# Attention into two feed-forward layers: scores and folds as tiles of the array, low weight bits on ScalarE

## Chip, cores and metric

One core of one Trainium2 chip runs the whole program. The metric is device microseconds for one execution, start to end; a smaller number is better. Engines: PE is TensorE (PEld its weight loads), DVE VectorE, ACT ScalarE, POOL GpSimd, SP the queue that issues nearly all DMAs.

## What is computed

```python
def _attn_ref(x, state):            # x (4,8,512,64), state (4,8,32,64)
    scale = 1.0 / np.sqrt(D)
    scores = scale * np.matmul(x, state.transpose(0, 1, 3, 2))
    scores = scores - scores.max(-1, keepdims=True)
    a = np.exp(scores)
    a /= a.sum(-1, keepdims=True) + 1e-09
    xread = np.matmul(a, state)
    scores2 = scale * np.matmul(state, x.transpose(0, 1, 3, 2))
    ...                             # the same softmax, over the 512 tokens
    sread = np.matmul(a2, x)
    return np.concatenate([xread, sread], axis=2)

h = X @ w_in1;  X2 = elu(h) @ w_out1            # X: (2304, 512)
h = X2 @ w_in2; out = (h * tanh(softplus(h))) @ w_out2
```

w_in is 512 x 2048 and w_out 2048 x 512, in both layers. They arrive as float64 and are read as pairs of 32-bit words.

## The kernel before

**Order.** The program hands some 1,800 operations to a planner (`Plan`, line 63). Each has an engine, a cost, a due time and the buffers it needs; `run` picks the next one by its own clock, so the order on each engine is fixed when the program is built. On the chip each engine and each DMA queue works strictly in that order.

**Weights** (`weight`, line 414). A piece of 128 x 512 float64 lands in `raw`. ACT scales the high words into `wy` (L446). DVE shifts `wy` left by three into `wv` (L455), ors in the top three bits of the low words (L457), and ors in the sign bit (L468, L474 or L478). There are 64 pieces, `raw_in` and `raw_out` of either layer. Most are then split into a rounded fp32r part and a remainder (`split_weight`, line 488), since the large products are made of three fp32r matmuls (L769 to L771, L849 to L851). The first eight steps of layer 1 use whole fp32 instead (L755, L837).

**Folds** (`fold`, line 509). For the tokens, attention output times w_in1 is written as probabilities times (state times w_in1). A fold makes `m`, state times w_in1, for one batch b and four pieces j. The array is cut into eight tiles of 64 x 32, one for each pair of head group and state half; a matmul covers two pieces (256 columns), so four pieces take two groups of eight products, which the planner may place apart. `m` leaves PSUM as fp32, and `fold_slice` (line 537) splits each piece of it into two halves of the tile `ms`, three steps before its use.

**Tokens** (`token_reads`, line 571), for each batch and half of the heads: x is turned on PE (L600), scores are eight 128-row products with a block-diagonal state `sd` of 64 columns (L638), softmax runs on DVE and ACT (L648 to L658), the probabilities are turned on PE (L663) and become `x1`. The raw scores go to DRAM (`s2d`, L654).

**States** (`state_reads`, line 674): the raw scores come back by DMA, x is loaded a second time with a column of ones (L566), a maximum over the tokens is taken on DVE (L685) and POOL (L686), and PE reads (L697).

**Stages.** Layer 1 works through four batches in sixteen steps each, with the 128 state rows as four more; layer 2 then has five blocks of rows, sixteen steps each. PE has eight PSUM banks: two `h`, four `acc`, two `att`, the last shared by everything of the attention and the folds. During the start (`early`) the others serve too.

```python
A("PE", 0.9, score, r=[(xT, q), ("sd", b, 0), ("sd", b, 1)], w=[(pt, q)], lag=lag, place=held)
add("ACT", 0.68, lambda: nc.scalar.activation(y.t, words()[0].bitcast(F32), AF.Copy, scale=2.0 ** -112),
add("DVE", 0.43, lambda: nc.vector.tensor_scalar(u32(v), u32(y), 3, None, ALU.logical_shift_left),
```

Of the kernel before, what the change touches and what calls it, by code (L numbers as in the profile page):

```python
# [40 lines left out]
class Buf:  # L41
# [7 lines left out]
    def __getitem__(self, i):  # L49
        return self.t[i]  # L50

# [5 lines left out]
class Plan:  # L57
# [59 lines left out]
    def run(self, take, dma):  # L117

        self.dues(dma)
        free = {}  # L120
# [15 lines left out]
        while todo:  # L136
# [52 lines left out]
            c = op.cost[e] if isinstance(op.cost, dict) else op.cost  # L189
            if e in dma:  # L190
# [25 lines left out]
def attention_elu_mish(  # L216
# [39 lines left out]
    negative = const.tile([P, 1], F32, name="negative")  # L256
    x2d = pools["dram"].tile([P, NK, NT * P], F32, name="x2d")
    w2d = pools["dram"].tile([P, 2, NF, DM], F32, name="w2d")
    s2d = pools["dram"].tile([P, B, 2, NC, P], F32, name="s2d")
# [77 lines left out]
    add("DVE", 2.8, make_ident, w=["ident"], due=-50.0)  # L337
    add("POOL", 0.1, lambda: nc.gpsimd.memset(one, 1.0), w=["one"], due=-50.0)
    add("POOL", 0.1, lambda: nc.gpsimd.memset(two, 2.0), w=["two"], due=-50.0)
    add("POOL", 0.1, lambda: nc.gpsimd.memset(negative, -0.0), w=["negative"], due=-50.0)  # L340

    banks = itertools.cycle(["att", "acc0", "att", "acc1", "h", "acc2", "h"] + ([] if FILL else ["acc3"]))
    early = True

    def bank(name):
        tag = next(banks) if early else "att"
# [17 lines left out]
    sd = [pools["at"].tile([P, 2, HH, 2, NS], F32, name=f"sd{b}") for b in range(B)]  # L364
# [11 lines left out]
    def load_states():  # L376
        raw = buf("w", "w_out", NF, [P, 2 * B, 2, D], F32, "st_raw")
        for i in range(2):
            A(ACTQ, 128.0, lambda i=i: nc.scalar.dma_start(
                out=raw[:, :, i, :], in_=state.rearrange("b (g h) n d -> (h n) (b g) d", g=2)),  # L380
              w=[(raw, i)], due=-50.0)
        for b in range(B):
            A("POOL", 0.5, lambda b=b: nc.gpsimd.memset(sd[b], 0.0), w=[("sd", b, i) for i in range(2)], due=-50.0 + b)
        st_raw.append(raw)

    def states(b0, b1):

        raw = st_raw[0]
        if True:
# [8 lines left out]
            for b in range(b0, b1):  # L398
                for i in range(2):
                    r = slice(i * D, (i + 1) * D)  # L400
                    A(EITHER, {"ACT": 0.41, "DVE": 0.43}, lambda e, b=b, b0=b0, i=i, r=r, pt=pt: copy(
                        e, sd[b][r, :, :, i, :],
                        pt[r, (b - b0) * 2 * P:(b - b0 + 1) * 2 * P].rearrange("p (g h n) -> p g h n", g=2, n=NS)),
                        r=[pt], w=[("sd", b, i)])
# [4 lines left out]
    def place_w1(j, k):  # L409
        return w1[j // 2].t.rearrange("p (k f) -> p k f", k=NK)[:, k, j % 2 * P:(j % 2 + 1) * P]  # L410
# [3 lines left out]
    def weight(kind, layer, j, due=None):  # L414
# [33 lines left out]
        signs = layer == 1 and Z_FROM <= j < Z_TO  # L448
        if signs:

            add("ACT", 0.68, lambda: nc.scalar.activation(v.t, y.t, AF.Identity, bias=negative, scale=2.0 ** -60),
                r=[y, "negative"], w=[v])
        else:

            add("DVE", 0.43, lambda: nc.vector.tensor_scalar(u32(v), u32(y), 3, None, ALU.logical_shift_left),  # L455
                r=[y], w=[v])
        add("DVE", 0.69, lambda: nc.vector.scalar_tensor_tensor(  # L457
            u32(v), words()[1], 29, u32(v), ALU.logical_shift_right, ALU.bitwise_or), r=[raw, v], w=[v])
        last = (3, ALU.logical_shift_left) if signs else (0x80000000, ALU.bitwise_and)
        if kind == "in" and layer == 1:  # L460
            if j // 2 not in w1:
                w1[j // 2] = buf("w", "w_in", NF, [P, NK * 2 * P], F32, f"w1_{j // 2}_")
            to = w1[j // 2]

            def sign():
                o = to.t.bitcast(U32).rearrange("p (k f) -> p k f", k=NK)[:, :, j % 2 * P:(j % 2 + 1) * P]
# [3 lines left out]
            add("DVE", 0.69, sign, r=[y, v], w=[(to, j % 2)])  # L470
            return
        if layer == 1 and j < WHOLE_OUT:
            w = w_sb["whole", layer, j] = buf("w", f"w_{kind}", NF, [P, DM], F32, f"whole{j}_")
# [12 lines left out]
    after_step = {}  # L486

    def split_weight(kind, layer, j, v):
        w = w_sb[kind, layer, j] = buf("w", f"w_{kind}", NF, [P, 2, DM], F32R, f"w_{kind}{layer}_{j}_")
# [573 lines left out]
```

## Time and profile before

| what | value |
|---|---|
| time, three runs | 752.93, 753.81, 754.55 us |
| span of the profiled execution, first to last instruction | 751.1 us |
| median less that span | 2.7 us |
| PE busy | 732.6 us, 98% |
| DVE, ACT, POOL busy | 556.8, 425.0, 10.6 us |
| moved by DMA | 81.71 MB |

The profiled execution's own time isn't listed beside the three, so the span stands for it and the 2.7 us for what lies around it. Busy time says how long an engine had something running; the chain of waits says which engine ended last at each moment.

### The profile page before, as it was taken

To read this page: it belongs to the slowest core of one execution; us is meant where nothing else is said; L and a number is where in the kernel's file an instruction comes from. 1 tells how busy PE (TensorE), PEld (TensorE's weight loads), DVE (VectorE), ACT (ScalarE), POOL (GpSimd) and SP (SyncE) were. 2 spreads that over 40 slices of the span, in tenths; PEclk is the share of its full clock that TensorE was granted. 3 is DMA by queue.
4 is the path that set the end of the run, shared out by engine and by line. 5 is a ranking of instruction groups with operands and counts; after the bars stand their busy time and mean duration, and the time that the engine had idled before them with its cause. 6 is when DMAs were issued, how large, how long until landed. Compare 5 with 4: busy or idle time off the path is not lost.

```text
span 751.1 us, 11051 instructions
## 1 busy us (share of the span) xinstructions
PE 732.6 (98%) x4098; PEld 598.0 (80%) x4098; DVE 556.8 (74%) x1048; ACT 425.0 (57%) x759; POOL 10.6 (1%) x27
## 2 busy tenths in 40 slices
PE   5899999999999999999999999999999999999996
PEld 5346677788777879878888888888889999999995
DVE  6988899988689895798999856565567565756564
ACT  3674767655567663577657445454455455545443
POOL 1000000010000000000000000000000000000000
PEclk8899999999999999999999999999999999999999
DMA  9953667453585543665845103000030020001001
GB/s 227 291 154 101 166 161 215 117 169 113 147 256 175 189 140 104 189 196 185 283 162 193 42 1 99 0 1 1 0 99 1 1 83 2 1 1 42 1 1 42
DMA packets 67292, 81.71 MB, mean 109 GB/s; under 512 B 22696, under 2 KB 45992, under 8 KB 67240
## 3 DMA queue, kind: packets, MB, share of 16 engines
q1 hardware_dynamic: 65028, 80.36, 36.1%
q10 hardware_dynamic: 2212, 0.66, 0.4%
q8 instruction: 32, 0.52, 0.3%
q14 instruction: 20, 0.16, 0.1%
HBM read 59.51 MB, written 21.50 MB: 108 GB/s over the span
## 4 chain that ended last, share of the span: by engine, by line
PE 94%; DMA 2%; DVE 1%; ACT 1%; issue 0%; SPq 0%; ACTq 0%
PE acc_acc L849 16%; PE acc_acc L851 15%; PE acc_acc L850 15%; PE h L769 12%; PE h L771 12%; PE h L770 12%; PE fold L523 2%; PE acc_acc L837 2%; PE h L745 2%; PE h L755 2%; DMA raw_in<-in_moe_w_in 2%; PE scores L638 1%; PE pT L663 1%; PE sr L697 1%; DMA xb<-in_x 1%; PE xT L600 1%
## 5 line engine op out<-in xcount | busy, mean ns | idle before, releaser
L788 ACT ACTIVATE e<-h 128x512 f32<-128x512 f32 (+1 forms) x148 | 83.2, 562 | 118.2 <-PE h L771 106.5
L813 ACT CAST g<-e 128x512 fp32r<-128x512 f32 (+1 forms) x142 | 82.4, 581 | 61.9 <-PE acc_acc L851 25.6
L771 PE MATMUL h<-x,w_in 128*128 128x384 f32 (+1 forms) x320 | 114.6, 358 | 0.0
L769 PE MATMUL h<-x,w_in 128*128 128x384 f32 (+1 forms) x320 | 114.4, 358 | 0.0
L770 PE MATMUL h<-x,w_in 128*128 128x384 f32 (+1 forms) x320 | 114.3, 357 | 0.0
L814 DVE TENSOR_TENSOR g<-e,g 128x512 fp32r<-128x512 f32 (+1 forms) x142 | 91.1, 642 | 22.5 <-ACT g L813 21.7
L851 PE MATMUL acc_acc<-w_out,g 128*128 128x512 f32 x272 | 106.9, 393 | 0.0
L850 PE MATMUL acc_acc<-w_out,g 128*128 128x512 f32 x272 | 106.7, 392 | 0.0
L849 PE MATMUL acc_acc<-w_out,g 128*128 128x512 f32 x272 | 105.9, 389 | 0.4 <-ACT g L813 0.4
L849 PE MATMUL acc_acc<-g,w_out 128*128 128x512 f32 x232 | 93.3, 402 | 0.0
L810 DVE TENSOR_TENSOR u<-u,e 128x384 f32<-128x384 f32 (+1 forms) x80 | 48.9, 611 | 57.7 <-ACT e L809 57.6
L850 PE MATMUL acc_acc<-g,w_out 128*128 128x512 f32 x232 | 90.5, 390 | 0.0
L851 PE MATMUL acc_acc<-g,w_out 128*128 128x512 f32 x232 | 90.5, 390 | 0.0
L808 ACT ACTIVATE e<-u,two 128x384 f32<-128x384 f32 (+1 forms) x80 | 52.8, 660 | 50.1 <-DVE u L806 49.9
L805 DVE TENSOR_SCALAR e<-e 128x384 f32<-128x384 f32 (+1 forms) x80 | 30.9, 387 | 48.2 <-ACT e L788 48.1
L769 PEld LDWEIGHTS h<-x,w_in 128*128 128x128 f32 x320 | 60.1, 188 | 7.1
L770 PEld LDWEIGHTS h<-x,w_in 128*128 128x128 f32 x320 | 60.1, 188 | 7.1
L771 PEld LDWEIGHTS h<-x,w_in 128*128 128x128 f32 x320 | 60.1, 188 | 5.0
L851 PEld LDWEIGHTS acc_acc<-w_out,g 128*128 128x128 f32 x272 | 51.0, 187 | 11.0 <-DVE g L814 0.3
L849 PEld LDWEIGHTS acc_acc<-w_out,g 128*128 128x128 f32 x272 | 51.1, 188 | 10.1 <-ACT g L813 0.9
L850 PEld LDWEIGHTS acc_acc<-w_out,g 128*128 128x128 f32 x272 | 51.0, 188 | 9.5
L849 PEld LDWEIGHTS acc_acc<-g,w_out 128*128 128x128 f32 x232 | 43.5, 188 | 13.5 <-issue 3.3
(126 smaller groups left out, 1169.7 us busy)
## 6 DMA issues: line engine op xcount, KB each, us to landing
raw_out<-in_moe_w_out SPq DMA_DIRECT2D x32, 512.0 KB, 4.3
raw_in<-in_moe_w_in SPq DMA_DIRECT2D x32, 256.0 KB, 7.3
raw_in<-in_moe_w_in SPq DMA_DIRECT2D x16, 512.0 KB, 4.2
w2d<-wv SPq DMA_DIRECT2D x32, 256.0 KB, 3.4
xb<-in_x SPq DMA_DIRECT2D x16, 256.0 KB, 4.2
x2d<-o SPq DMA_DIRECT2D x16, 256.0 KB, 2.6
xb<-in_x SPq DMA_DIRECT2D x32, 128.0 KB, 3.9
back_in<-w2d SPq DMA_DIRECT2D x16, 256.0 KB, 3.0
```

The source lines that it names most:

```text
L769: nc.tensor.matmul(h[:, :n], lhsT=wh, rhs=xh, start=(k == 0), stop=False)
L770: nc.tensor.matmul(h[:, :n], lhsT=wh, rhs=xl, start=False, stop=False)
L771: nc.tensor.matmul(h[:, :n], lhsT=wl, rhs=xh, start=False, stop=(k == nk - 1))
L788: add("ACT", act(n), lambda: nc.scalar.activation(E(), Hh(), AF.Exp), r=[h], w=[e])
L805: add("DVE", 0.1 + 0.00065 * n, lambda: nc.vector.tensor_scalar(E(), E(), E20, None, ALU.min), r=[e], w=[e])
L808: add("ACT", act(n) + 0.12, lambda: nc.scalar.activation(E(), U(), AF.Ln, bias=two), r=[u, "two"], w=[e])
L810: add("DVE", dve(n), lambda: nc.vector.tensor_tensor(U(), U(), E(), ALU.mult), r=[u, e], w=[u])
L813: add("ACT", act(n) + 0.01, lambda: nc.scalar.copy(g[:, 0, :n], E()), r=[e], w=[(g, 0)])
L814: add("DVE", dve(n), lambda: nc.vector.tensor_tensor(g[:, 1, :n], E(), g[:, 0, :n].bitcast(F32), ALU.subtract), r=[e, (g, 0)], w=[(g, 1)])
L849: nc.tensor.matmul(acc.t, lhsT=st[:, 0, :], rhs=mv[:, 0, :], start=fst, stop=False)
L850: nc.tensor.matmul(acc.t, lhsT=st[:, 0, :], rhs=mv[:, 1, :], start=False, stop=False)
L851: nc.tensor.matmul(acc.t, lhsT=st[:, 1, :], rhs=mv[:, 0, :], start=False, stop=lst)
```

## The change

- **Weights**: ACT makes the low three bits from the low words, as integers (`wv`), beside `wy`. DVE's shift by three goes; DVE ors sign and low bits, then the shifted `wy`.
- **Folds**: `w1` is laid out in fours, and a fold is one group of eight products of 512 columns. For all but the first eight steps it leaves PSUM as a rounded copy and a DVE subtraction from PSUM (L549 of the new kernel); `fold_slice` goes.
- **Scores**: eight products on tiles of 64 x 32, each 256 columns wide. Turns of 32 x 32 blocks on DVE (L620, L625, L640, L646) replace PE's turn of the probabilities.
- **States**: the raw scores and x stay in SBUF, so `s2d`, the second load of x, the ones and POOL's reduction go. One DVE maximum, POOL's 128x1 scaling, one ACT exponential that also sums, and a PE turn (L673) of the result with its copy come in. State copies are 4 of 128x256 in place of 8 of 64x256.
- **Planner**: other constants and gates for state reads, a start offset, and slower PE costs in its first 16 us; `w_in`, `w_wide` and `w_out` buffers are cut otherwise.

```diff
+        add("ACT", 0.68, lambda: nc.scalar.activation(
+            u32(v), words()[1], AF.Copy, bias=-0.5, scale=2.0 ** -29 * (1 - 2.0 ** -20)), r=[raw], w=[v])
         add("DVE", 0.69, lambda: nc.vector.scalar_tensor_tensor(
-            u32(v), words()[1], 29, u32(v), ALU.logical_shift_right, ALU.bitwise_or), r=[raw, v], w=[v])
-        last = (3, ALU.logical_shift_left) if signs else (0x80000000, ALU.bitwise_and)
+            u32(v), u32(y), 0x80000000, u32(v), ALU.bitwise_and, ALU.bitwise_or), r=[y, v], w=[v])
+        last = (3, ALU.logical_shift_left)
...
-        step = min(2, j1 - j0)
+        step = j1 - j0
...
+            A(EITHER, both(n), lambda g, e=e: copy(g, ms[0][:, e, :], pts[e].t), r=[(pts[e], j0)], w=[(ms[0], e)])
+            A("DVE", 0.69, lambda e=e: nc.vector.tensor_tensor(
+                ms[1][:, e, :], pts[e].t, ms[0][:, e, :].bitcast(F32), ALU.subtract),
+              r=[(pts[e], j0), (ms[0], e)], w=[(ms[1], e)], lag=0.5)
-        add(EITHER, {"ACT": 0.41, "DVE": 0.33}, lambda e: copy(e, t[:, 0], src()), r=keys, w=[(t, 0)])
-        add("DVE", 0.43, lambda: nc.vector.tensor_tensor(t[:, 1], src(), t[:, 0].bitcast(F32), ALU.subtract),
...
+        def score_tiles():
+            for h in range(HH):
+                for t in range(2):
+                    r, l = slice(t * D, (t + 1) * D), slice(h * NS, (h + 1) * NS)
+                    nc.tensor.matmul(ps[t][l, 0:2 * P], lhsT=sd[b][r, hf, h, :],
+                                     rhs=xT[r, h // 2, h % 2 * 2 * P:(h % 2 + 1) * 2 * P],
+                                     start=True, stop=True, tile_position=(t * D, h * NS))
...
+            if early:
+                A("DVE", 0.43, lambda t=t: nc.vector.transpose(
+                    pr()[:, t * 2 * P:(t + 1) * 2 * P], ps[t][:, 0:2 * P]), r=[ps[t]], w=[(kp, t)])
+            A(EITHER, both(2 * P), lambda e, t=t: copy(e, krv()[:, t, :], ps[t][:, 0:2 * P]), r=[ps[t]], w=[krk(t)],
...
+            A("DVE", 0.69, lambda: nc.vector.transpose(pr(), krv().rearrange("p t f -> p (t f)")),
...
-        A(SP, 256.0, lambda: nc.sync.dma_start(out=s2d[:, b, hf], in_=raw()), r=[kr], w=[("s2d", b, hf)])
...
-        A("PE", NC * 0.11, turn2, r=["ident", kp], w=[p2], lag=lag, place=[xt])
+        back = lambda o, i: nc.vector.transpose(
+            o.rearrange("p (c t f) -> p t c f", c=2, t=2), i.rearrange("p (t c f) -> p t c f", t=2, c=2))
...
-        xb = load_x_ones(b, hf)
+        xb, raw, rawk = kept.pop((b, hf))
...
-        A("POOL", 1.2, lambda: nc.gpsimd.partition_all_reduce(tot.t, col.t, P, RMAX), r=[col], w=[tot], lag=1.0)
+        A("POOL", 0.3, lambda: nc.gpsimd.tensor_scalar(top.t, top.t, SCALE, None, ALU.mult), r=[top], w=[top])
+        A("ACT", 0.8, lambda: nc.scalar.activation(
+            raw(), raw(), AF.Exp, bias=top.t, scale=SCALE, accum_out=den.t), r=[top],
+        A("PE", NC * 0.11, turn, r=["ident", *rk], w=[pe], lag=1.0, place=[exT])
+        A(EITHER, both(S), lambda e: copy(e, exT.t.rearrange("p c f -> p (c f)"), pe.t), r=[pe], w=[exT], lag=1.0)
```

**VectorE's order, from the first scores to the last piece of x1 of batch 0.** `mx` and `sm` are the softmax's maxima and sums, `prob` the probabilities of either half of the heads, `w_0` the layer-1 weight. Before:

```order
L648 TENSOR_REDUCE mx_196<-scores_193 128x16
L649 TENSOR_TENSOR prob_194<-scores_193,mx_196 128x512
L648 TENSOR_REDUCE mx_219<-scores_217 128x16
L649 TENSOR_TENSOR prob_218<-scores_217,mx_219 128x512
L655 TENSOR_REDUCE sm_197<-prob_194 128x16
L656 TENSOR_SCALAR sm_197<-sm_197 128x16
L657 RECIPROCAL sm_197<-sm_197 128x16
L655 TENSOR_REDUCE sm_220<-prob_218 128x16
L658 TENSOR_TENSOR prob_194<-prob_194,sm_197 128x512
L656 TENSOR_SCALAR sm_220<-sm_220 128x16
L657 RECIPROCAL sm_220<-sm_220 128x16
L658 TENSOR_TENSOR prob_218<-prob_218,sm_220 128x512
```

Now:

```order
L636 TENSOR_SCALAR sm_162<-sm_162 128x16
L637 RECIPROCAL sm_162<-sm_162 128x16
L638 TENSOR_TENSOR prob_159<-prob_159,sm_162 128x512
L635 TENSOR_REDUCE sm_198<-prob_196 128x16
L636 TENSOR_SCALAR sm_198<-sm_198 128x16
L457 SCALAR_TENSOR_TENSOR wv_226<-wy_222,wv_226 128x512
L637 RECIPROCAL sm_198<-sm_198 128x16
L640 STREAM_TRANSPOSE x_0_6_240<-prob_159 128x2x2x128
L638 TENSOR_TENSOR prob_196<-prob_196,sm_198 128x512
L468 SCALAR_TENSOR_TENSOR w_0_28_217<-wy_222,wv_226 128x4x128
L640 STREAM_TRANSPOSE x_0_6_240<-prob_196 128x2x2x128
L457 SCALAR_TENSOR_TENSOR wv_232<-wy_229,wv_232 128x512
```

The turn into x stands on DVE now, and two instructions of a weight (L457, L468) stand among the last five of the softmax.

**ScalarE's order at the same place.** Before:

```order
L446 ACTIVATE wy_203<-raw_in_1_33_131 128x512
L275 COPY sd_82<-st_169 64x8x32
L446 ACTIVATE wy_225<-raw_in_2_40_134 128x512
L275 COPY prob_218<-scores_217 128x512
L651 ACTIVATE prob_194<-prob_194 128x512
L651 ACTIVATE prob_218<-prob_218 128x512
```

Now:

```order
L634 ACTIVATE prob_159<-prob_159 128x512
L453 ACTIVATE wy_222<-raw_in_1_33_124 128x512
L455 ACTIVATE wv_226<-raw_in_1_33_124 128x512
L453 ACTIVATE wy_229<-raw_in_2_40_143 128x512
L455 ACTIVATE wv_232<-raw_in_2_40_143 128x512
L634 ACTIVATE prob_196<-prob_196 128x512
```

Both pieces of weight 1 and of weight 2 now stand ahead of the second half's exponential.

## Rows read from the trace of the kernel before

**Rows 1.** The page: busy time of each engine, and the chain by engine.

```profile
PE 732.6 (98%) x4098; PEld 598.0 (80%) x4098; DVE 556.8 (74%) x1048; ACT 425.0 (57%) x759; POOL 10.6 (1%) x27
...
PE 94%; DMA 2%; DVE 1%; ACT 1%; issue 0%; SPq 0%; ACTq 0%
```

**Rows 2.** Busy time by stretch: stretch, length, busy us (instructions), PE clock, DMA.

```profile
20.00:30.00 10.00, 8.30 (x65) 4.00 (x66) 9.48 (x19) 5.39 (x12) 0.00 (x0) 0.80 1.09 273
...
80.00:90.00 10.00, 8.57 (x40) 7.05 (x38) 8.60 (x17) 6.43 (x13) 0.00 (x0) 1.00 0.52 124
340.00:360.00 20.00, 20.00 (x90) 16.57 (x89) 18.73 (x37) 16.16 (x29) 0.00 (x0) 1.00 0.57 175
```

**Rows 3.** What PE waited for: total us, times, longest.

```profile
PE pT L663 <- DVE sm L656: 1.6, 1, 1.6
PE h L769 <- DVE e L798: 1.4, 1, 1.4
...
PE fold L523 <- ACT m L275: 0.6, 1, 0.6
```

**Rows 4.** Order of time at the start, ScalarE: start, us, instruction, [idle before].

```profile
11.19 0.67 ACT L446 ACTIVATE wy<-raw_in 128x512 f32<-128x512 f32 x1 [0.80 <-DMA raw_in<-in_moe_w_in]
...
13.60 0.66 ACT L446 ACTIVATE wy<-raw_in 128x512 f32<-128x512 f32 x1 [0.95 <-DMA raw_in<-in_moe_w_in]
...
16.04 0.67 ACT L446 ACTIVATE wy<-raw_in 128x512 f32<-128x512 f32 x1 [1.38 <-DVE mx L648]
```

**Rows 5.** The chain, start to the first product: start, us, what.

```profile
18.76 0.60 DVE sm L655
19.60 0.25 DVE sm L657
...
21.14 1.09 PE pT L663 x4
...
23.32 2.16 PE h L755 x4
```

**Rows 6.** Groups by line: busy, mean ns of one, idle before.

```profile
L446 ACT ACTIVATE wy<-raw_in 128x512 f32<-128x512 f32 x32 | 21.4, 673 | 8.9 <-DMA raw_in<-in_moe_w_in 5.9 <-DVE mx L648 1.4 <-DVE wv L478 1.4
L455 DVE TENSOR_SCALAR wv<-wy 128x512 uint32<-128x512 uint32 x64 | 27.1, 425 | 5.3 <-ACT wy L446 3.1 <-DMA w2d<-wv 2.0
L478 DVE SCALAR_TENSOR_TENSOR wv<-wy,wv 128x512 uint32<-128x512 uint32 x42 | 28.8, 685 | 0.3
L331 DVE STREAM_TRANSPOSE ident_rows<-ident_cols 128x32 f32<-128x32 f32 x1 | 0.2, 211 | 0.0
```

**Rows 7.** The chain in the stage where PE is full: start, us, what.

```profile
42.25 1.72 PE h L755 x4
43.97 3.43 PE acc_acc L837 x8
...
77.25 0.59 PE fold L523 x16
77.84 0.43 PE h L769
...
119.41 0.24 PE acc_acc L850
...
120.57 1.02 PE fold L523 x32
...
175.98 0.44 PE pT L663 x4
176.42 1.73 PE scores L638 x16
178.15 0.28 PE h L769
```

**Rows 8.** Order of time, ScalarE at 50 us: one instruction behind another.

```profile
51.21 0.39 ACT L275 CAST ms<-m 128x256 fp32r<-128x256 f32 x1
51.50 0.68 ACT L446 ACTIVATE wy<-raw_out 128x512 f32<-128x512 f32 x1
```

More of the change, by code (lines that the diff above doesn't have):

```diff
@@ L119, in run @@
         self.dues(dma)
-        free = {}
+        free = dict.fromkeys(("PE", "DVE", "ACT", "POOL", *dma), READY_AT)
         ready = {}
@@ L398, in states @@
             for b in range(b0, b1):
[L399 to L404, printed above, removed]
+                A(EITHER, both(2 * P), lambda e, b=b, pt=pt: copy(
+                    e, sd[b].rearrange("p g h n -> p (g h n)"), pt[:, (b - b0) * 2 * P:(b - b0 + 1) * 2 * P]),
+                  r=[pt], w=[("sd", b)])
     w1, w_sb, w_back = {}, {}, {}
     def place_w1(j, k):
-        return w1[j // 2].t.rearrange("p (k f) -> p k f", k=NK)[:, k, j % 2 * P:(j % 2 + 1) * P]
+        return w1[j // NC][:, k, j % NC * P:(j % NC + 1) * P]
     loads = itertools.count()
@@ L652, in token_reads @@
-        A(EITHER, both(S), lambda e: copy(e, raw().rearrange("p c f -> p (c f)"), pt.t), r=all_c, w=[kr],
-          due=T[index[1, b, 0]] + (15.0 if early and LATE else -8.0))
-        A(SP, 256.0, lambda: nc.sync.dma_start(out=s2d[:, b, hf], in_=raw()), r=[kr], w=[("s2d", b, hf)])
-        A("DVE", 0.69, lambda: nc.vector.tensor_reduce(sm.t, prg(), AX.X, ALU.add), r=[kp], w=[sm])
+        ps = [bank("scores", f"acc{2 * hf + t}") for t in range(2)]
+        def score_tiles():
[5 more added lines that the diff above has]
+                                     start=True, stop=True, tile_position=(t * D, h * NS))
@@ L665, in token_reads @@
-        A("PE", NC * 0.11, turn2, r=["ident", kp], w=[p2], lag=lag, place=[xt])
+        A("DVE", 0.69, lambda: nc.vector.tensor_tensor(prg(), prg(), wide(sm), ALU.mult), r=[sm], w=keys,
+          place=[xt])
+        back = lambda o, i: nc.vector.transpose(
+            o.rearrange("p (c t f) -> p t c f", c=2, t=2), i.rearrange("p (t c f) -> p t c f", t=2, c=2))
         if not b:
-            A(EITHER, both(S), lambda e: copy(e, xt[:, hf, :], p2.t), r=[p2], w=[(xt, hf)], lag=ahead)
+            A("DVE", 0.69, lambda: back(xt[:, hf, :], pr()), r=keys, w=[(xt, hf)], lag=ahead)
@@ L749, in mm1 @@
                 A("PE", 4 * mm(4 * P), f, w=[h], due=due,
-                  r=[(w1[sl // 2], sl % 2)] + [("sread", b) for b in range(B)])
+                  r=[(w1[sl // NC], sl % NC)] + [("sread", b) for b in range(B)])
         elif kind == 1 and (blk, j) in WHOLE:
@@ L986, in attention_elu_mish @@
         begin(min(WHOLE_J, 4), split_first)
-    for s in range(first2):
-        if steps[s][0] == 1 and (steps[s][1], steps[s][4]) not in WHOLE:
-            begin(s - 3, fold_slice, s)
     for s in range(len(steps) + 2):
```

248 lines of the change are left out of this document (110 added, 138 removed).

## Prediction

> **What bounds the kernel now.** I read the page's chain first, then the stretches, then what PE waited for. The chain that ended last lies on PE for 94% of the span, and PE is busy for 98% [rows 1]. At 340 to 360 us PE is full at full clock while DVE and ACT have idle time [rows 2]: from there on only the work on PE counts, and the change leaves that part of PE's work as it is. Two places differ. Before the first product at about 23 us PE waits for the first softmax and the first weights: the chain there runs through DVE, then two turns at 1.09 us each (0.44 each later, at full clock), then the first product [rows 5, 7], and at 20 to 30 us the granted clock is 0.80 on average and PE is busy for 8.30 of 10 us [rows 2]. And at 80 to 90 us PE is busy for only 8.57 us, with one wait of 1.4 us behind a DVE instruction [rows 2, 3]. So the change is worth what it takes off PE after 23 us, what it takes off the start, and what it adds in waits.
>
> **The start.** The first half of x1 needs the second DVE turn (L640), the second half one more. I follow the new order. Weight 0 has landed by 11.19 us, weight 1 by 13.60, and weight 2 by 16.04 at the latest, where ACT was waiting for DVE [rows 4]. Two ACT instructions per weight cost 0.67 + 0.58 = 1.25 us if they follow each other, since the next one starts some 0.1 us before the last has ended (0.29 us after a start of 0.39 us) [rows 6, 8]. Weight 2 then holds ACT until 17.3 us, and the second exponential behind it until 17.9. DVE goes on with the sum (0.60), the small addition and reciprocal (about 0.4), one instruction of weight 1 (0.6), the first turn (0.6): the first half of x1 is there at about 20.1 us. Multiplication, L468 and second turn take 1.8 more: 21.9. PE takes the first half from 20.2 to 21.9 at the low clock (1.72 us for four instructions at full clock [rows 7], so 0.86 per half, twice that at 1.2 GHz), then the second fold, and ends the first product at about 24.3. Before, it ended at 23.32 + 2.16 = 25.5 [rows 5]. **-1.2 us.**
>
> The unknown in this is the 512-wide turn on DVE. The trace has one of 32 columns: 211 ns [rows 6]. Below, it costs a one-source copy, 0.43 as L455; above, 16 times the row, 3.4. I take 0.69, as other 512-wide DVE instructions (685) [rows 6], because at 1 ns for each of 32 columns the row leaves about 0.18 us of fixed cost, which is that value again for 512. The Trainium skill's "Vector Engine (DVE) Microarchitecture Reference" (The reshape front-end and per-opcode configuration) says that the transposing array sustains one element per cycle and lane; by that it is an estimate of 0.7 us, and the sum is the same.
>
> **Scores.** Six halves (batches 1 to 3) are computed while PE is full. Each takes 1.73 us now, and the next instruction 0.28 in place of 0.24 [rows 7]. The new form, eight products of 256 columns on 64x32 tiles, is what a half fold is: 0.59 us, and the next full-array instruction takes 0.43 [rows 7]. So 1.77 becomes 0.78, six times: **-5.9 us.** Batch 0's scores lie in the start.
>
> **Turns.** The probabilities' turns leave PE (0.44 for a half [rows 7]), and turns of the exponentials come, 0.44 again. Six of the old ones, but all eight of the new, lie in the full stretch: **+0.9 us.** State reads themselves stay, with 64 columns for 65.
>
> **Folds.** A group of 32 takes 1.02 us and one of 16 takes 0.59 [rows 7]: 0.43 per 16 instructions and 0.16 fixed. With the 0.19 on the next instruction, each separate stretch of folding costs 0.35. The columns are the same in sum, so I price 512-wide products by columns; the order shows 21 stretches before and 18 now. **-1.05 us.** The unknown here is a fixed cost per product, which could add up to 0.1 us to a group or take that off.
>
> **Waits that go.** The 1.4 us wait and the 0.6 us one [rows 3] lie behind DVE and ACT work on m and on its slices; these slices (56 pairs of small instructions) become 28 pairs of 512 columns straight from PSUM. **-2.0 us.** What is late next is the bank: a fold now holds both `att` banks until DVE's subtractions are done, and the next turn or score on PE waits for that. In the order I find this at the second group of batch 0 (a turn of x right behind a fold) and at the scores of batch 1, each worth 0.3 to 0.6 us. I take **+1.0 us**, between none and 3.
>
> **What hides.** DVE loses 64 x 425 ns = 27.2 us (L455) [rows 6] and the slices, and gains turns and copies: about 30 us less. ACT gains 64 x 0.673 = 43.1 us and loses some 12 of slices. Both have room: at 20 to 30 us ACT is busy 5.39 of 10 us [rows 2]. Where ACT is fullest, between the first ELU and step 4, the order has 40 ACT instructions, 24 of them for twelve weights: 25.7 us by face duration, 22 with the overlap, against 23.9 of PE work (four products of 1.72, four of 3.43 [rows 7], 3.3 of folds and turns). It just fits, so I price it at nothing. On that row (673 against 425 ns) the Trainium skill's "ScalarE: Activation LUTs" (Rules for kernel authors) speaks against the move: adding and multiplying belong on VectorE. By it the sum would be 64 x 0.25 = 16 us worse if ACT set the end; by the trace PE sets it, and the move costs nothing.
>
> DMA: 48 issues fewer on SP, 16 of them 256 KB and 32 of 128 KB, all away from the end; at 80 to 90 us the engines are half busy [rows 2]. Nothing. But x now stays in its buffer until its state read; three buffers serve six halves, and the gates put each read before the load that needs its place. POOL's work becomes eight tiny instructions. Nothing.
>
> **Sum:** -1.2 - 5.9 + 0.9 - 1.05 - 2.0 + 1.0 = -8.25 us against the span of 751.1: 742.9. The median of the runs shown is 2.7 above that span: **745.6 us.**
>
> **Rivals.**
> 1. *ACT becomes the bound from 24 to 50 us.* If its instructions don't overlap, 25.7 against 23.9 us puts PE 1.8 us behind, and four copies that PE waits for (folds and scores) come one ACT instruction (0.6) late each: 4.2 us, 749.8. For it: the near balance. Against: the overlap [rows 8], and slack of over 1 us before each ELU result that I followed. Should the integer output cost more than the scaling does, each 0.1 us adds 1.2; at a doubled 1.34 us the whole gain is gone (no change). What the skill's rule says would come this way.
> 2. *The clock.* PE does less before 20 us, and the granted clock, which in the trace came back only after PE had worked from 21.1 on (0.80 over 20 to 30 us [rows 2]), may come back 3 us later. Work of 1.5 us then takes 3: 747.1. The Trainium skill's "TensorE: Matmul & The Clock Gate" (What's actually happening) agrees that the clock is withheld until there is activity.
> 3. *Slower: the DVE turns are dear.* The start has four of 256 and two of 512 columns in line on DVE, four 512-wide turns in all. At 16 blocks of 211 ns, 3.4 us, each is 2.7 dearer: +10.8, 756.4. It decides from 0.69 + 8.25/4 = 2.75 us a turn. Against: the row of 32 columns covers four blocks of 32 rows at once, so blocks are not serial in that direction.
> 4. *The scores don't run side by side.* At 0.43 us a product, eight in a row take 3.4 us: six times 2.9 more than forecast, 763. The fold's row, same tiles and width, speaks against it.
>
> **Chances.** Forecast 0.65; ACT 0.16; clock 0.12; turns 0.05; scores in a row 0.02. A measurement here tells apart 0.2%, 1.5 us, so faster is below 752.3. Forecast, clock and 0.11 of ACT are faster: 0.88. The rest of ACT, with dearer integers, is no change: 0.05. Turns and scores are slower: 0.07. The range goes from 741.5 (no new waits, and the second fold hidden, and two more us from the start's other gaps) to 751, which takes in rival 2 and rival 1 with the spread of the runs.
>
> **What would show it.** Right: scores at about 0.6 us a half and PE's busy time some 8 us less; the first product ended by 24 to 25 us; no PE wait over 1 us after it; ACT over 9 tenths from 25 to 50 us without PE waiting; turns of 512 columns at 0.7 us. Wrong: PE waits for ACT copies or for ELU before 60 us, a first product later than 25.5 us, or a clock of 0.5 beyond 25 us.

## The result, and the profile after

| | before | after |
|---|---|---|
| median | 753.61 us (4 runs, 752.93 to 754.55) | 744.15 us (4 runs, 743.26 to 744.95) |
| span of the profiled execution | 751.1 us | 743.2 us |
| DVE, ACT, POOL busy | 556.8, 425.0, 10.6 us | 532.1, 448.0, 2.7 us |
| moved by DMA | 81.71 MB | 73.28 MB |

The ratio is 0.9874, 95% interval 0.986 to 0.9888: 9.5 us less on the medians, 7.9 on the spans. The forecast was 745.6 us. One execution of e9 below took 1865.65 us and is left out of its median; all others lie within 1% of the fastest of their kernel.

The medians and the spans differ because of the executions that were profiled. Around its span a run of the changed kernel has 1.8 us (744.95 less 743.2; the other three have 1.8 as well). The span of 751.1 before therefore belongs to a run of about 752.9, the fastest of its four, and the one after to 744.95, the slowest of its four. So the 2.7 us of "median less that span" were 1.8 around the span and 0.9 between that run and the median, and the 7.9 us that the traces can place are 1.6 less than the medians show.

PE's busy time and the chain, from the page after (before: [rows 1]):

```profile
PE 723.5 (97%) x3874; PEld 580.2 (78%) x3874; DVE 532.1 (72%) x955; ACT 448.0 (60%) x796; POOL 2.7 (0%) x14
...
PE 95%; DVE 2%; ACT 1%; DMA 1%; issue 0%; ACTq 0%
```

PE is still the engine that counts, with 9.1 us less work. Stretches after, columns as in [rows 2]:

```profile
20.00:30.00 10.00, 9.28 (x57) 3.22 (x58) 6.78 (x13) 5.70 (x12) 0.00 (x0) 0.66 1.09 286
24.00:25.00 1.00, 1.00 (x3) 0.48 (x2) 0.48 (x1) 0.10 (x1) 0.00 (x0) 0.50 1.01 397
26.00:27.00 1.00, 1.00 (x2) 0.34 (x1) 0.37 (x1) 1.00 (x3) 0.00 (x0) 0.62 1.11 268
80.00:90.00 10.00, 10.00 (x76) 8.06 (x75) 9.06 (x16) 7.23 (x13) 0.00 (x0) 1.00 0.28 63
340.00:360.00 20.00, 20.00 (x90) 16.58 (x89) 15.85 (x27) 14.79 (x26) 0.00 (x0) 1.00 0.71 218
```

At 80 to 90 us PE is now full (8.57 before). At 20 to 30 us it works more (9.28 for 8.30), but at a mean clock of 0.66 for 0.80: the granted clock is 0.50, which is 1.2 GHz, up to 26 us; before, it was back by 24. At 340 to 360 us PE is full as it was.

What PE waited for, total us, times, longest ([rows 3]):

```profile
PE fold L535 <- ACT sd L289: 3.2, 1, 3.2
...
PE fold L535 <- DVE w L468: 2.9, 1, 2.9
PE h L742 <- DVE x L640: 1.4, 1, 1.4
...
PE fold L535 <- ACT m L289: 0.5, 1, 0.5
```

The waits of 1.4 us behind DVE at 80 us and 1.6 behind the softmax have gone. The wait of a fold for ACT's copy of `m`, 0.6 us before, is still there (0.5). The long ones lie ahead of the first product or end with it; behind it none is longer than 0.5 us.

The chain around the first product, start, us, what ([rows 5]):

```profile
19.49 0.58 DVE x L640
20.07 0.14 issue
20.21 2.04 PE h L742 x2
22.25 0.61 PE fold L535 x16
22.86 4.73 PE h L742 x6
```

The first half of x1 leaves DVE at 20.07 us, the product starts at 20.21. Its second half is the first two of the six instructions, 1.7 us at 1.2 GHz, so it ends at 24.6 us (25.5 before).

The chain further on, with the pieces that answer to [rows 7]:

```profile
53.68 0.59 PE scores L613 x16
54.27 1.06 PE h L742 x2
...
85.99 0.44 PE exT L673 x4
...
98.28 1.02 PE fold L535 x16
99.30 0.43 PE acc_acc L836
```

A half of the scores takes 0.59 us, where it took 1.73, and the pair of products behind it 1.06, where such a pair takes 0.86. A turn of exponentials takes 0.44. A fold of 512 columns takes 1.02 for 16 records, as 32 of 256 columns did.

Groups by line, busy us, mean ns of one, idle before ([rows 6]):

```profile
L455 ACT ACTIVATE wv<-raw_out 128x512 uint32<-128x512 uint32 x32 | 21.3, 667 | 1.2 <-DVE w_out L500 1.1
L455 ACT ACTIVATE wv<-raw_in 128x512 uint32<-128x512 uint32 x32 | 21.2, 663 | 0.0
...
L535 PE MATMUL fold<-w,sd 64*32 64x512 f32 x224 | 15.3, 601 | 0.5 <-ACT m L289 0.5
...
L640 DVE STREAM_TRANSPOSE pT<-prob 128x512 f32<-128x512 f32 x6 | 4.3, 710 | 0.3
...
L535 PE MATMUL fold<-w,sd 64*32 64x256 f32 x48 | 2.0, 388 | 0.0
```

The integer output costs ACT what the scaling does, and a turn of 512 columns on DVE 0.71 us.

**Where the 7.9 us went.** The first matmul on the state read starts at 286.03 us before and at 278.12 after: the whole 7.9 us has been gained by then, and behind it both kernels keep PE full for 451.6 us. The gain lies in two parts: 0.9 us up to the end of the first product, and 7.0 from there on, of which 6.1 are work of PE (258.2 us before, 252.1 after) and 0.9 idle time of PE (2.3 and 1.4). The low clock takes part of this back: the last four of the six instructions shown, from 24.6 to 27.59 us, take 3.0 us, where four take 1.72 at full clock [rows 7].

### The profile page after: what moved, and what is told of

The parts are those of the page before. It is cut to its first block, busy times and chain, and to the rows that moved or that the text cites. A ratio compares the mean times of both kernels' runs of the same rounds, so it can differ in the third digit from the quotient of the medians.

```text
span 743.2 us, 10373 instructions
## 1 busy us (share of the span) xinstructions
PE 723.5 (97%) x3874; PEld 580.2 (78%) x3874; DVE 532.1 (72%) x955; ACT 448.0 (60%) x796; POOL 2.7 (0%) x14
## 2 busy tenths in 40 slices
DMA packets 48090, 73.28 MB, mean 99 GB/s; under 512 B 5544, under 2 KB 28840, under 8 KB 48040
## 4 chain that ended last, share of the span: by engine, by line
PE 95%; DVE 2%; ACT 1%; DMA 1%; issue 0%; ACTq 0%
PE acc_acc L836 16%; PE acc_acc L838 15%; PE acc_acc L837 15%; PE h L756 12%; PE h L758 12%; PE h L757 12%; PE acc_acc L824 3%; PE h L742 2%; PE fold L535 2%; PE h L732 2%; DMA st_raw<-in_state 1%; PE xT L601 1%; PE sr L684 1%; PE acc_att L837 0%; PE acc_att L836 0%; PE acc_att L838 0%
## 5 line engine op out<-in xcount | busy, mean ns | idle before, releaser
L785 DVE SCALAR_TENSOR_TENSOR e<-e,h 128x512 f32<-128x512 f32 x62 | 42.3, 683 | 27.3 <-ACT e L778 27.2
L758 PE MATMUL h<-x,w_pair 128*128 128x384 f32 (+1 forms) x160 | 57.3, 358 | 0.0
L758 PE MATMUL h<-x,w_in 128*128 128x384 f32 (+1 forms) x160 | 57.3, 358 | 0.0
L756 PE MATMUL h<-x,w_pair 128*128 128x384 f32 (+1 forms) x160 | 57.3, 358 | 0.0
L756 PE MATMUL h<-x,w_in 128*128 128x384 f32 (+1 forms) x160 | 57.3, 358 | 0.0
L757 PE MATMUL h<-x,w_in 128*128 128x384 f32 (+1 forms) x160 | 57.2, 357 | 0.0
```

The costliest lines, as they stand in the source:

```text
L756: nc.tensor.matmul(h[:, :n], lhsT=wh, rhs=xh, start=(k == 0), stop=False)
L757: nc.tensor.matmul(h[:, :n], lhsT=wh, rhs=xl, start=False, stop=False)
L758: nc.tensor.matmul(h[:, :n], lhsT=wl, rhs=xh, start=False, stop=(k == nk - 1))
L785: add("DVE", dve(n), lambda: nc.vector.scalar_tensor_tensor(E(), E(), -1.0, Hh(), ALU.mult, ALU.max), r=[e, h], w=[e])
```

## The experiments

All times are medians; before stood at 753.4 to 753.9 us beside them. The last column is against the changed kernel's 744.15, which was not run again beside them. Traces are of one execution of each run. The planner lays its order anew whenever costs, operations or constants change, so most of these runs change the order too. The traces show where it stays: in e3, e8 and e12 the instructions of DVE, ACT and the DMA queue come in the changed kernel's order, and in e5 they do until behind the first product.

| run | what | us | ratio to before (95%) | against after |
|---|---|---|---|---|
| e1 | before, scores in tiles | 754.0 | 1.0004 (0.9995 to 1.0014) | +9.9 |
| e7 | before, low bits on ACT | 753.35 | 0.9994 (0.9986 to 1.0003) | +9.2 |
| e11 | before, new planner constants | 753.36 | 1.0002 (0.9994 to 1.0011) | +9.2 |
| e2 | after, low bits on DVE | 749.31 | 0.9938 (0.9926 to 0.9951) | +5.2 |
| e4 | after, scores twice | 748.03 | 0.9919 (0.9906 to 0.9933) | +3.9 |
| e5 | after, folds planned 256 wide | 749.37 | 0.9946 (0.9927 to 0.9965) | +5.2 |
| e12 | after, folds 256 wide, same order | 744.48 | 0.9884 (0.9871 to 0.9897) | +0.3 |
| e6 | after, old planner constants | 752.8 | 0.9994 (0.9982 to 1.0005) | +8.6 |
| e9 | after, old transfer model | 750.98 | 0.9963 (0.9948 to 0.9977) | +6.8 |
| e10 | after, old read gates | 745.47 | 0.9897 (0.9885 to 0.991) | +1.3 |
| e3 | after, PE kept busy, 12 | 745.33 | 0.9885 (0.9871 to 0.9898) | +1.2 |
| e8 | after, PE kept busy, 7 | 745.31 | 0.9882 (0.9863 to 0.99) | +1.2 |

### One part alone: scores in tiles (e1)

```diff
-TILES_FROM = 4
+TILES_FROM = 1
```

The kernel before holds an older form of the tiles; this uses it for batches 1 to 3.

> The kernel before, with scores on eight tiles for batches 1 to 3 alone (copied out and turned back on PE, so everything behind them is as before). Theory, the sum by PE's work: each of six halves falls from 1.77 to 0.78 us and gains a turn of 0.44: 6 x 0.55 = 3.3 us off 753.6, 750.3. Rival, the scores lay beside waits of PE anyway: no change. Rival, the gain came from DVE and ACT work and not from PE: no change, or slower, since two copies come in.

Measured: 754.0 us, no change, where a gain was expected. PE does the six halves faster (0.59 us and a turn of 0.44, for 1.73), and loses it at the second state read, in order of time, [idle before] last:

```profile
123.57 1.09 DVE L685 TENSOR_REDUCE col<-scores 128x128 f32<-128x512 f32 x1 [1.00 <-DMA scores<-s2d]
124.83 0.73 POOL L686 PARTITION_ALL_REDUCE tot<-col  x1 [6.61 <-DVE col L685]
126.44 0.68 DVE L687 TENSOR_TENSOR scores<-scores,tot 128x512 f32<-128x512 f32 x1
127.64 0.62 ACT L689 ACTIVATE scores<-scores 128x512 f32<-128x512 f32 x1
128.17 0.56 ACT L275 COPY m<-fold 128x512 f32<-128x512 f32 x1
128.83 0.66 PE L697 MATMUL sr<-xb,scores 128*32 128x65 f32 x32 [2.42 <-issue]
```

PE arrives earlier and stands 2.42 us in front of the chain through DRAM, DVE, POOL and ACT. The exponential ends at 128.26 us; what ends last before PE starts is ACT's copy of a fold out of its bank, in line behind the exponential, at 128.73. In the kernel before the same exponential ended at 127.26 us, and PE came to that read only at 129.79, so nobody saw the chain. The change takes this chain out (the exponentials are turned on PE, and nothing goes through DRAM).

The wait costs more than itself. Behind it PE runs at 1.2 GHz; the granted clock is third from last:

```profile
129.00:130.00 1.00, 1.00 (x34) 0.81 (x26) 0.93 (x5) 0.48 (x2) 0.13 (x1) 0.84 0.08 33
130.00:131.00 1.00, 1.00 (x4) 0.81 (x3) 1.00 (x3) 0.00 (x0) 0.00 (x0) 0.50 0.46 102
```

The clock is back at 133 us, so some 1.7 us of PE's work there are lost as well. Wait and clock together are 4.1 us, more than the 3.3 that the scores save; the wait of 1.4 us at 80 us, now 0.4, gives 1.0 back. In the execution that was profiled (755.04 us, 1.0 above the median) the clock was also low until 27 us at the start. That is not the edit's doing, since the order of PE, DVE, ACT and the DMA queue is that of the kernel before up to there.

### One part alone: low bits on ACT (e7), and the other way round (e2)

```diff
...
-            add("DVE", 0.43, lambda: nc.vector.tensor_scalar(u32(v), u32(y), 3, None, ALU.logical_shift_left),
-                r=[y], w=[v])
+        add("ACT", 0.68, lambda: nc.scalar.activation(
+            u32(v), words()[1], AF.Copy, bias=-0.5, scale=2.0 ** -29 * (1 - 2.0 ** -20)), r=[raw], w=[v])
...
```

> The kernel before with one part of the change alone: ScalarE makes the low three bits of each weight. Theory A (DVE is in line at the start and behind the waits of 1.4 and 0.6 us, so its relief gains by itself): 753.9 less 1.0 (two to three of the 0.43 us instructions out of line before the first product) less 2.0 of waits, 750.9 (750.0 to 752.2). Theory B (relief of DVE gains only where PE has become short enough to reach the next wait; in the old order other waits stand behind it): 753.2 to 754.6, no difference. Theory C (ACT becomes the bound): over 755, with ACT at 10 of 10 us somewhere between 20 and 60 us and PE waiting for ACT.

Measured: 753.35, no difference (theory B). The waits that a relief of DVE was to end are still there, of the same size; one of PE's waits, and the stretch it lies in:

```profile
PE h L762 <- DVE e L791: 1.4, 1, 1.4
```

```profile
80.00:90.00 10.00, 8.57 (x51) 6.71 (x52) 9.26 (x18) 8.28 (x15) 0.77 (x2) 1.00 0.63 175
```

The reverse, the lines above with - and + exchanged in the changed kernel:

> The changed kernel with the low bits made on DVE again (shift, then or), ACT's second instruction gone; all else stays. Theory, PE sets the end and the move hides: 743 to 746, against 744.2. Rival, DVE's relief of 27 us carries part of the gain: 747 or more. Rival, ACT is held up by its 43 us more in the first 60 us: 742.5 or less.

Measured: 749.31, 5.2 us over the changed kernel: the rival, and not the theory. PE in order of time, one instruction of DVE, and the stretches:

```profile
20.78 2.04 PE L742 MATMUL h<-x,m 128*128 128x512 f32 x2 [5.53 <-DVE x L640]
...
50.09 1.23 PE L601 MATMUL xT<-ident,xb 128*128 128x128 f32 x8 [2.25 <-issue]
```

```profile
49.30 1.28 DVE L549 TENSOR_TENSOR m<-fold,m 128x512 fp32r<-128x512 f32 x2
```

```profile
30.00:50.00 20.00, 17.84 (x54) 7.50 (x40) 19.43 (x36) 13.22 (x22) 0.00 (x0) 1.00 0.78 211
50.00:100.00 50.00, 48.95 (x312) 31.12 (x313) 46.07 (x86) 33.09 (x60) 0.90 (x2) 1.00 0.36 93
```

The wait of 5.53 us in front of the first product looks dear and isn't: it takes the place of two waits with a fold between them (3.2 and 1.4 in the changed kernel), the product starts 0.57 us later, and the fold behind it at 26.98 us, for 27.52. The loss comes later. DVE is full at 30 to 50 us (19.43 of 20) and PE is not (17.84; 19.48 in the changed kernel, with DVE at 18.34). A fold holds both `att` banks until DVE has subtracted. Here DVE comes to that only at 49.30 us, for a fold that PE ended at 30.4, and the turn of x on PE starts behind the first of the two, at 50.09; in the changed kernel DVE subtracts from 40.10 us on, and the turn at 43.65 waits for nothing. The profile doesn't name what ended the 2.25 us; that it was the bank is read from these times. Between first product and state product PE is idle for 4.7 us, 3.3 more than in the changed kernel (this execution took 748.93, 4.0 more than the changed kernel's). The same 27 us of DVE's work that are worth nothing in the old kernel are worth 5.2 in the new one, with the orders that the planner makes of each: DVE's and ACT's differ from 12 us on, and how much of the 5.2 is order and how much DVE's load isn't shown.

### The size of the scores' term (e4)

```diff
-            for h in range(HH):
+            for h in (*range(HH), *range(HH)):
```

(and the operation's cost, 0.65 to 1.08, in the planner.) The scores are made twice, with the same values.

> The changed kernel with each half's scores computed twice into the same banks: 16 products in place of 8. Theory: a second pass adds the columns only, 0.43 us, six times while PE is full, and up to 0.9 at the start: 2.6 to 3.5 us slower, 746.8 to 747.7. Rival, tiles don't run side by side or a pass has its own fixed cost of 0.35: 4.7 us or more. Rival, PE has room: no change.

Measured: +3.9 us, a little over the upper end. The halves in the chain:

```profile
54.07 1.02 PE scores L613 x32
55.09 1.05 PE acc_acc L824 x2
```

0.43 us more for each of eight halves is 3.4 us, 2.6 of them for the six behind the first product. The execution that was profiled took 747.15, the fastest of four. In it the first product starts 0.7 us later (20.91) and the 256-wide fold behind it 0.8 us earlier than in the changed kernel (26.74 for 27.52), so the start loses nothing. From that fold to the state product (280.20 for 277.96, both in order of time) it takes 3.0 us longer: 2.6 for the scores, and a wait for ELU of 1.1 in place of 0.4. So time of PE there goes into the end about one for one. The median lies 1.7 us further up than this trace shows; a size can't be read from such a run to better than that.

### The width of the folds (e5, e12)

```diff
-        step = j1 - j0
+        step = min(2, j1 - j0)
```

> The changed kernel, with its folds made of products of 256 columns in place of 512. The order has 21 stretches of folding then (12 of 16 products, 9 of 8), as before the change, where the changed kernel has 18. My step: a fold costs by its columns, and a stretch by itself 0.35 us, so 3 x 0.35 = 1.05 us more than the changed kernel: 745.2 us (744.7 to 746.0). Rival A, a fixed cost per product that the wide form saves: 0.1 us for each of 14 wide groups more, 746.6. Rival B: the width costs nothing on PE, and what comes free is taken up at once: 744.2, no difference.

Measured: +5.2 us, off all three figures by far. The trace says that it is no answer on the width. It is of the slowest of six executions (753.02; the others took 747.83 to 750.30). PE in order of time:

```profile
10.28 1.09 PE L404 MATMUL st<-ident,st_raw 128*128 128x128 f32 x4 [3.06 <-DMA st_raw<-in_state]
...
24.30 2.05 PE L742 MATMUL h<-x,m 128*128 128x512 f32 x2 [2.30 <-DVE x L640]
```

The first product starts at 24.30 us for 20.21, and the order isn't the reason: on every engine and queue it is the changed kernel's up to there. PE had to wait for the state's load until 10.28 us (7.38 in the changed kernel), though it is issued at 0.75 us in both, so 2.9 of the 4.1 us are a late landing in this one execution. Behind the first product the order is another, and PE is idle for 3.6 us up to the state product (1.4). What the other five executions lost, no trace shows. So the width was tried again with the planner's operations left as they are:

```diff
-            for k in range(NK):
...
+            wide = min(2, step) * P
+            for q in range(0, step * P, wide):
+                for k in range(NK):
...
```

> The changed kernel in its own order, with each fold product of 512 columns issued as two of 256 within the same planned operation, so that nothing but the width on PE changes (the earlier run with 256-wide folds also changed the planner's operations, and with them the order of the start). Theory (folds cost by columns, 1.02 us for 16 of 512 as for 32 of 256): 744.0 to 744.6. Rival: a fixed cost of 30 to 100 ns per product, which 112 more products on four tiles side by side would show as 14 groups x 0.1 = 1.4 us: 745.0 to 745.8.

Measured: 744.48, +0.3 with overlapping intervals. The fold's group:

```profile
L537 PE MATMUL fold<-w,sd 64*32 64x256 f32 x496 | 17.4, 383 | 0.5 <-ACT m L289 0.5
```

17.4 us, where the changed kernel has 15.3 for 512 columns and 2.0 for 256. The width costs PE nothing; folds go by columns.

### The planner's constants (e6, e9, e10, e11)

The change also alters how the planner reckons. First all of it was put back:

```diff
-        free = dict.fromkeys(("PE", "DVE", "ACT", "POOL", *dma), READY_AT)
+        free = {}
...
-GATE_READS, GATE_SECOND = (6, 8, 12, 15, 24, 28, 35, 38), 14
-BACKLOG, RATE = 3.0, 245.0
-READY_AT, COLD_UNTIL, COLD = 0.75, 16.0, 1.35
+GATE_READS, GATE_SECOND = (10, 14, 18, 22, 26, 30, 34, 38), 14
+BACKLOG, RATE = 3.0, 330.0
+READY_AT, COLD_UNTIL, COLD = 0.75, 0.0, 1.0
```

> The changed kernel, with the planner's constants of before (engines free from time 0, no dearer PE work before 16 us, the load gates 10, 14, 18, ... 38, a link of 330, latency 2.0). Theory: the start is set by the data (weights' landing, then DVE's chain to x1), not by these constants: within 0.8 us of the changed kernel, 743.4 to 745.0, first product ended between 24.0 and 25.4 us. Rival: the constants carry part of the gain, since the order of the first 40 loads decides which weight ACT waits for: 746 to 750, with a PE wait of over 1.5 us on weights or folds before 60 us that the changed kernel has not.

Measured: 752.8 us. The whole gain is gone, and the theory with it; the time lies even above the rival's 750, and the waits are for x and ELU, not for weights. PE's longest waits behind the first fold:

```profile
PE xT L601 <- DMA xb<-in_x: 3.9, 1, 3.9
...
PE h L756 <- DVE e L785: 2.1, 1, 2.1
```

Behind both the granted clock falls to 0.50, at 32 to 34 us and at 84 to 86. So the constants were put back apart. The transfer model alone:

```diff
-BACKLOG, RATE = 3.0, 245.0
+BACKLOG, RATE = 3.0, 330.0
...
-        plan.run(take, {SP: (0.6, RATE, 2.2), ACTQ: (0.6, RATE, 2.2)})
+        plan.run(take, {SP: (0.6, RATE, 2.0), ACTQ: (0.6, RATE, 2.0)})
```

> The changed kernel with the planner's transfer model of before alone (a link of 330 KB a microsecond and a latency of 2.0, for 245 and 2.2); its other constants stay new. Theory (the planner orders PE's queue by when it believes x of batch 1 to have landed; at 330 it puts that batch's turns ahead of the second group of folds, where the run with all the old constants waited 3.9 us for x and lost the clock to 1.2 GHz behind it): 748 to 752.5, with a PE wait of 3 to 4 us on the turn of x at 27 to 32 us. Rival A: the gates of the state reads or the dearer early PE work carried the 8.6 us; then 744 to 745.5 here. Rival B: both halves, 746 to 748.

Measured: 750.98, +6.8, as the theory has it; the six executions spread from 748.1 to 752.0. PE in order of time, then stretches with PE's clock third from last:

```profile
28.20 0.66 PE L535 MATMUL fold<-w,sd 64*32 64x256 f32 x16
32.99 1.94 PE L601 MATMUL xT<-ident,xb 128*128 128x128 f32 x8 [4.12 <-DMA xb<-in_x]
34.72 1.86 PE L742 MATMUL h<-x,m 128*128 128x512 f32 x2
```

```profile
32.00:33.00 1.00, 0.01 (x1) 0.04 (x1) 0.00 (x0) 1.00 (x3) 0.00 (x0) 0.99 1.09 348
33.00:34.00 1.00, 1.00 (x5) 0.86 (x6) 0.00 (x0) 0.86 (x2) 0.00 (x0) 0.50 1.15 229
34.00:36.00 2.00, 2.00 (x7) 1.40 (x6) 1.85 (x3) 0.00 (x0) 0.00 (x0) 0.50 1.12 221
```

At 330 KB a microsecond the planner puts the turns of x of batch 1 right behind a fold, ahead of the next products, and all four loads of x one behind another (two and two in the changed kernel). DMA moves 220 to 350 KB a microsecond in this stretch; PE reaches the turns at 28.9 us, stands in line behind x for 4.1, and comes out of the idle time at 1.2 GHz. In the changed kernel's order the first of these turns stands behind another fold and 32 instructions of products, at 43.65 us. The start is later too (first product at 22.16 us for 20.21). The old kernel had the same rate at no cost, because its turns of batch 1 come only at 53 us.

> The changed kernel with the state reads begun at the steps of before (10, 14, 18, ... 38) in place of (6, 8, 12, 15, 24, 28, 35, 38). These act from 60 us on, where PE is full. Theory (only the start counts): 743.7 to 745.0. Rival: a read that begins later holds x's buffer longer, so a later x load and its scores come late, and PE waits 1 to 3 us for ELU or x at 80 to 90 us, as the run with all the old constants did for 2.1 us: 745.5 to 748.

```diff
-GATE_READS, GATE_SECOND = (6, 8, 12, 15, 24, 28, 35, 38), 14
+GATE_READS, GATE_SECOND = (10, 14, 18, 22, 26, 30, 34, 38), 14
```

Measured: 745.47, +1.3, at the rival's lower bound: the wait for ELU goes from 0.4 to 1.0 us, and PE's busy time at 70 to 80 us from 9.63 to 9.04. 6.8 and 1.3 make 8.1 of the 8.6 us, each good to about a microsecond or two. Little is left for the free times and the dearer early PE work, the rest of the constants; they weren't run alone.

The transfer model and those two in the kernel before (without the gates):

```diff
-        free = {}
+        free = dict.fromkeys(("PE", "DVE", "ACT", "POOL", *dma), READY_AT)
...
-BACKLOG, RATE = 3.0, 330.0
+BACKLOG, RATE = 3.0, 245.0
```

> The kernel before with the planner's new constants alone (link 245 and latency 2.2, engines free from 0.75 us, PE work before 16 us by 1.35). Theory (they keep the changed kernel's shorter chain from waiting for x; the old kernel turns x of batch 1 only at 53 us, long after it has landed, and has no such wait to lose): 753.0 to 754.6. Rival: the constants gain by themselves, as the difference of 8.6 us in the changed kernel would suggest: 745 to 750.

Measured: 753.36, no difference, as the theory has it.

### What the low clock costs (e3, e8)

PE has little to do from 12 to 20 us (busy for 1.28 of 8), and the clock is at 1.2 GHz from 13 us until 26. Spare products of the identity, in one of the `h` banks, were to fill the gap; 12 operations of four products, then 7 (which the planner counts at 0.93 us each):

```diff
...
+    def idle(n=4):
+        for i in range(n):
+            nc.tensor.matmul(spare[:, i % 4 * P:(i % 4 + 1) * P], lhsT=ident, rhs=ident, start=True, stop=True)
...
+    last_op = score_ops[-1]
+    for i in range(BUSY):
+        last_op = add("PE", 0.6, idle, r=["ident"], w=[spare], due=1e6, after=[last_op])
...
+BUSY = 12
```

> The changed kernel with spare products of the identity on PE, between the scores of batch 0 and the first product, into a bank that nobody reads. Theory, the low clock from 20 to 26.6 us costs: with the full clock the work that took 6.4 us takes less, and what is left waits for the second half of x1 at 21.9 us: 2 to 3 us faster, 741.2 to 742.2, if the clock stays up. Rival, DVE and ACT set the pace there (weights, ELU of step 0), so that PE waits for them: 0.5 us or less.

Measured: 745.33, where 741.2 to 742.2 was expected. The clock is 1.00 throughout, but the spare operations take 0.93 us each and push the first product to 23.53 us. With 7:

> The changed kernel with 7 spare PE operations in place of the 12 of the run before (0.93 us each there; in the order 5 stand before the first fold and 2 between it and the first product). Theory (the clock falls because PE has nothing to do from 12 to 20 us, and costs 1.5 to 3 us; the 12 delayed the first product by 3.3 us and so gave it back): the 5 end at 16.8 us, the 2 at about 20.5, the clock stays at 1.00 throughout, the first product starts at 20.3 to 20.8 at full clock and ends at 22.7 to 23.4 in place of 24.6, in all 742.2 to 743.0 us. Rival A: the clock falls in the gap from 16.8 to 18.1 us all the same, and the time is that of the changed kernel or up to 0.8 worse: 744.2 to 745.0. Rival B: an earlier first product only meets the weights' landing and DVE's chain behind it (a fold at 27.5 us in both kernels): 744.0 to 744.5 with the clock at 1.00.

Measured: 745.31 us. The start went as the theory has it, and the time didn't; what happened is Rival B's case, at a time 0.8 us above its bound. On PE the first product now starts at 20.77 us at full clock, and the fold behind it stands at 25.25 us, for 27.52 in the changed kernel: 2.3 us of lead. Where it goes, stretches and then one instruction of ACT:

```profile
36.00:40.00 4.00, 4.00 (x10) 1.71 (x9) 0.58 (x1) 1.09 (x2) 0.00 (x0) 1.00 0.99 305
40.00:44.00 4.00, 2.17 (x8) 0.80 (x6) 3.78 (x7) 4.00 (x9) 0.00 (x0) 1.00 0.45 160
```

```profile
38.91 0.68 ACT L453 ACTIVATE wy<-raw_in 128x512 f32<-128x512 f32 x1 [4.27 <-DMA raw_in<-in_moe_w_in]
```

At 36 to 40 us ACT and DVE have next to nothing to do: ACT waits 4.27 us for a weight, while the DMA engines are busy 0.99 of the time. PE runs out of work at 40 to 44 us (2.17 of 4), and the state product starts at 278.06 in order of time, 277.96 in the changed kernel. The trace is of one execution (745.05). The six spread from 742.2 to 747.3, the changed kernel's four from 743.3 to 745.0; what the faster and slower ones did isn't shown. Neither of the two is shown to be a better kernel.

## Why the prediction was right

The forecast was 745.6 us and 744.15 was measured. Its sum of -8.25 stands against -7.9 on the spans and -9.5 on the medians. Point by point:

- **Start, -1.2.** -0.9. The product starts at 20.2 us as forecast. Its end was off by 0.3, and by then the second 128-wide fold (0.6 us at the low clock) has been done, which stood behind the first product before.
- **Scores, -5.9.** 0.59 for a half and 0.20 on the next instructions, as forecast; e4 shows that time on PE there goes into the end.
- **Turns, +0.9.** 0.44 each in the chain, as forecast.
- **Folds, -1.05.** 20.4 us in all before (18.6 for the 256-wide and 1.8 for the 128-wide records), 19.3 after (15.3, 2.0 and 2.0). That a fold goes by columns was an assumption; e12 bears it out. With the same 496 instructions e12's folds cost 17.4 us, for 18.6 before, so the gain comes from fewer separate stretches, as the prediction has it.
- **Waits, -2.0 and +1.0.** PE's idle time between the first product and the state product fell by 0.9 us, for 1.0 forecast. The total is right partly by luck. Of the two waits that were to go, the one of 1.4 us went and the one of 0.6 stayed (0.5, a fold behind ACT's copy of `m`). Of the two bank waits that were to come, the turn of x has one of 0.5 us and the scores of batch 1 have none; PE also waits 0.4 us for ELU. The reason given was too simple as well. I put it down to the work on m that leaves DVE and ACT; e7 shows that relieving DVE by 27 us ends no wait in the old order, and e10 that part of it hangs on when a state read is begun.
- **Rivals 1, 3 and 4.** ACT was busy 9.40 of 10 us at 30 to 40 and 17.32 of 20 at 30 to 50, and PE waited for no copy of it by more than 0.5; a 512-wide turn on DVE took 0.71 us, a half of the scores 0.59. None of the three came.
- **Rival 2, the clock.** It happened, from 24 to 26 us, and I gave it 0.12 as something that moves the time. One of my signs of being wrong, a clock of 0.5 beyond 25 us, came with a time that was right. The product behind the first took PE 1.3 us more by it, for 1.5 in this rival. Keeping the clock up (e8) was worth 2.3 us at 25 us and nothing at 45, because the next weights hadn't landed. This rival's price was read from PE alone; the step that failed is that a delay at 25 us counts in full. The Trainium skill's "TensorE: Matmul & The Clock Gate" (What's actually happening) has activity release the clock; e3 and e8 agree (1.00 throughout with spare work), but a full clock there wasn't worth time.
- **"What hides": DVE's relief, priced at nothing.** This was wrong as a part of the changed kernel: without it, and in the order that the planner then makes, the time is 5.2 us longer (e2). Half of my sentence holds, that the move to ACT costs nothing (e7). The other half says that both engines have room, and its row has room for ACT alone: at 20 to 30 us DVE was busy for 9.48 of 10 us [rows 2]. In e2 it has none at 30 to 50 (19.43 of 20), and the bank that a fold holds, a term of 0.3 to 0.6 us in the forecast, then costs 2.25. DVE's time fell by 24.7 us and ACT's rose by 23.0, for about 30 each. The Trainium skill's "ScalarE: Activation LUTs" (Rules for kernel authors) would leave such work on VectorE. It speaks of the price of an element, and per instruction the trace agrees (425 ns there [rows 6], 663 to 667 here); the kernel is no slower for the move (e7), and 5.2 us slower without it (e2).
- **What had no term.** The planner's constants were in the forecast only through the new order, which I followed. They decide over 8.6 us (e6), nearly all of the gain, and a forecast from the changed operations that took no account of the order would have been the same for both.

Taken together: the work that left PE is what the sum says, but three parts of the change put alone into the old kernel give nothing (e1, e7, e11), and taking one out of the new one costs 1.3 to 8.6 us (e10, e2, e9, e6). At 20 to 130 us the kernel stands close to several limits at once (PE, DVE, the landing of weights and x, and in the old one the chain through DRAM), and each part alone only moves PE to the next of them. That is read from the traces of e1 and e7. Another reading is open: the old constants may suit the old operations and the new ones the new, and no part was put into the old kernel together with constants chosen for it.

What stays open: the 6.1 us less work of PE are close to the forecast's -5.9 + 0.9 - 1.05 = -6.05 by two things that it didn't have. The low clock costs 1.3, the fold that now lies ahead of the first product's end gives some 0.45 back, and what gives back the other 0.9 is not placed in any term. The 1.6 us by which the medians differ more than the spans lie in executions without a trace, and so does the reason why some executions of e5, e8 and e9 are faster than others.

## What to carry to other kernels

When an engine is bound by a narrow margin, ask of each saving which wait it runs into next; parts of a change can be worth nothing alone and a lot together. A program order that is set by an estimate of transfers is part of the kernel's speed: one instruction placed 4 us ahead of its load held PE for as long, and the clock fell with it (e9). To measure the cost of a width or a form, hold the order fixed, or the run measures the order as well. Before a trace is taken for a run's explanation, see where its execution lies among the others: the traces of e5 and e1 begin late with the same order. And a long wait is not yet a loss: compare when the engine comes out of it (e2).

## What the runs showed of the hardware

- A full clock at the start was worth nothing in the execution traced: PE kept at 2.4 GHz (1.00 from 9 to 30 us) only reached the wait for a weight sooner (e8).
- PE was idle from 28.9 to 33.0 us (e9) and took up its work at 1.2 GHz, where the clock had been granted in full up to 33 us; the turns and products behind it ran at half speed up to 36 us. The same followed a wait of 2.42 us in e1 (0.50 from 130 to 133 us), and not one of 2.25 us in e2 (1.00 at 50 to 55).
- The state's load, issued at 0.75 us in both, was there for PE at 7.38 us in the changed kernel's trace and at 10.28 in e5's.
- DVE turns a 128 x 512 fp32 tile in 0.70 to 0.71 us, next to 0.68 for a subtraction of that width, and ACT writes integers at the price of floats (0.663 to 0.667 us, next to 0.669 to 0.673).
- On 64 x 32 tiles products cost by columns: 496 records of 256 took 17.4 us (e12), the same columns as 224 of 512 and 48 of 256 took 17.3 (the changed kernel).
